# A new order of units, output halves, softmax pieces and bands in the first four blocks of a fused dynamic convolution and squared-ReLU feed-forward kernel

## Chip, cores and metric

The kernel runs on one core of one Trainium2 chip. The metric is the device time of one execution in microseconds (us). In the profile lines PE is TensorE, ACT ScalarE, DVE VectorE and POOL GpSimd.

## The reference

```python
w = softmax(weight_gen, axis=-1)          # (8, 4096, 8 heads, 7 taps)
x_pad = pad x (8, 4096, 192) with 6 zero rows in front
y[b, s, h, :] = sum_k w[b, s, h, k] * x_pad[b, s + k, h, :]   # 24 channels a head
h = maximum(y.reshape(32768, 192) @ w_in, 0)                  # w_in 192 x 2048
out = (h * h) @ w_out                                         # w_out 2048 x 192
```

## The kernel before

The 32768 rows are cut into sub-blocks of 512 rows. Blocks 0 and 1 are one sub-block each, all later blocks are two. For each block there are these kinds of work:

- **Softmax pieces** give the taps: an exponential on ScalarE ("E"), then sum, reciprocal and scaling on VectorE ("S"). The inputs come in numbered parts; "part 1's weights" below are the softmax inputs of part 1, not weights of the feed-forward. The taps of small parts are moved into the row layout by DMA ("row moves"); those of large parts go through a buffer v_big, which is cleared once.
- **Bands** ("B"): VectorE spreads the taps of a sub-block over a band matrix, so that the convolution is a matmul.
- **Convolution** ("C"): TensorE multiplies x with the bands into one or two tiles "yp", and ScalarE casts them to y.
- **Units** ("u"): the first matmul of 2 x 512 values into a tile h of PSUM (three such buffers, shared with yp), a relu on ScalarE into t (five buffers), a square on VectorE into g.
- **Halves** ("M"): a quarter is 256 rows of out, and a half is half of its second matmul. After the second half ScalarE copies the sum out, and if the quarter used two banks, VectorE adds the second bank.

W_in and w_out are the weights of the two matmuls. In the traces each engine does its work in program order: in run 1 below, for instance, a relu whose unit had ended at 18.90 us began only at 21.93, behind an exponential that stood before it and waited 1.25 us for its weights. So the order written in the program is the schedule. In blocks 0 to 3 it was this:

```python
orders = {0: "uuuuuCuuu", 1: "MuMuuuMuuuMCu", 2: "MuuuuMuuuuMuuuuuuuMCu"}
steady = "MuMuuu" * 3 + "MuuuMCu"          # from block 3 on
# softmax pieces and bands hang on a unit: (block, unit)
at(0, 4, "exp", s1, 0, s1.rh)
at(0, 5, "soft", s1, 0, s1.rh)
...
st_conv(0)
st_bands(1)
x_cast(1, nc.vector.tensor_copy)
nc.gpsimd.memset(x_st[1][:, 0:1], 0.0)     # a gate: waits for the cast of x
for q in range(4):
    load_w_out(q, 4)
s2.load(nc.gpsimd)
nc.gpsimd.memset(v_big, 0.0)
...
for j, (sub, n) in enumerate(BLOCKS):
    u = m = 0
    for step in orders.get(j, steady):
        if step == "M":                    # a half of block j - 1
            qt, part = divmod(m, 2)
            m += 1
            if part == 0:
                o = new_o(ps_o, 1 if j < 3 else 2)   # one bank (128 rows) or two (64 rows each)
            st_mm2(j - 1, qt, FCS[part], (0, 1), o)
            if part == 1:
                o_sum(j - 1, qt, (0, 1), o)
                ...
        elif step == "u":
            run_fill(j, u)
            st_unit(j, u)
            u += 1
        elif j + 1 < NBLK:
            st_conv(j + 1)
    if j == 0:
        x_load(2)                          # on GpSimd's queue, behind the row moves
        x_load(3)
```

The softmax here doesn't subtract the row's maximum and nothing guards it: scores larger than these inputs give would overflow.

## Time and profile before

| | before |
|---|---|
| median time, 3 runs | 751.88 us (751.43 to 752.27) |
| profiled span | 749.2 us |
| TensorE busy | 739.0 us (99%) |
| VectorE, ScalarE busy | 621.8 and 623.0 us (83% each) |
| mean granted clock | 1.000 |
| blocks 0 to 4 begin at | 15.47, 24.14, 38.92, 57.66, 80.59 us |

"Busy" of TensorE counts a matmul that waits inside a group (7 units of block 2 count as 5.55 us of work without a gap, where they take 4.5 at the price of 0.65 each), so 99% does not mean that nothing is lost. What is lost shows when the starts of the blocks are compared with the price of the work in them. The prediction below does this and prints the lines. Two words of the profile: "<-" in brackets names what ended a wait, and "issue" is a wait for which the profile shows no cause.

### The profile page before, as it was taken

Reading aid. Unit: us, or ns where it says so; the run is one execution under the profiler, and the core shown is the slowest. Engines: PE = TensorE matmul, PEld = TensorE weight load, DVE = VectorE, ACT = ScalarE, POOL = GpSimd, SP = SyncE. Lnnn points to the kernel's source line nnn. Section 1 sums busy time; section 2 is a strip of 40 time slices with the busy share of each in tenths; the row PEclk is TensorE's granted clock in tenths of the full one; section 3 lists DMA queues with packets and bytes.
Section 4 is the critical chain, followed back from the end, with each engine's and each line's share of the span. In section 5 each row is a group of like instructions: output and inputs, shape, how many; then the busy total and the mean of one; then the engine's idle time right before and its main releaser. Section 6 shows DMA issues by size and latency. Waiting matters only on the chain.

```text
span 749.2 us, 33282 instructions
## 1 busy us (share of the span) xinstructions
PE 739.0 (99%) x15106; PEld 559.8 (75%) x15106; DVE 621.8 (83%) x1001; ACT 623.0 (83%) x753; POOL 87.9 (12%) x127
## 2 busy tenths in 40 slices
PE   8899999999999999999999999999999999999998
PEld 4658777777887777777877777777778777777787
DVE  5889998998789888887888888898888987677853
ACT  4898888888888888888888888888888888888883
POOL 3522220001101000011000110001100011001000
PEclk9999999999999999999999999999999999999999
DMA  8846444446453344543245442365441354441312
GB/s 231 129 74 135 79 68 109 101 78 138 93 109 69 74 77 80 131 86 65 46 80 139 86 80 49 55 138 108 59 79 47 57 109 80 59 75 50 50 45 65
DMA packets 122329, 65.20 MB, mean 87 GB/s; under 512 B 83881, under 2 KB 118668, under 8 KB 121676
## 3 DMA queue, kind: packets, MB, share of 16 engines
q1 hardware_dynamic: 77868, 46.05, 22.4%
q0 software_dynamic: 44176, 16.93, 20.6%
q8 instruction: 118, 1.93, 1.1%
q14 instruction: 23, 0.19, 0.1%
q10 hardware_dynamic: 144, 0.10, 0.0%
HBM read 48.61 MB, written 28.70 MB: 103 GB/s over the span
## 4 chain that ended last, share of the span: by engine, by line
PE 88%; DVE 5%; DMA 3%; ACT 1%; issue 1%; SPq 0%; POOL 0%; DVEq 0%; ACTq 0%
PE o L453 42%; PE h L419 40%; PE yp L394 6%; DVE g L431 2%; DVE bd L326 1%; DMA xt<-in_x_dram 1%; ACT t L428 1%; DMA x_st<-in_x_dram 1%; DMA vd<-v_big 1%; DVE v_first L217 1%; DVE ssum L202 0%; DVE rcp L209 0%; DMA wg<-in_weight_gen_dram 0%; DVE o_sb L469 0%; POOL wr L308 0%
## 5 line engine op out<-in xcount | busy, mean ns | idle before, releaser
L428 ACT ACTIVATE t<-h 128x1024 f16<-128x1024 f32 x512 | 497.1, 1027 | 66.9 <-PE h L419 66.6
L431 DVE TENSOR_TENSOR g<-t 128x1024 f16<-128x1024 f16 x512 | 334.5, 687 | 101.9 <-ACT t L428 99.1
L453 PEld LDWEIGHTS <-g 64*128 64x128 f16 (+1 forms) x8032 | 353.0, 94 | 55.7 <-issue 5.0
L453 PE MATMUL o<-w_o,g 64*128 64x192 f16 (+1 forms) x8032 | 386.1, 243 | 1.7 <-DMA w_o<-in_moe_w_out_dram 0.7
L419 PE MATMUL h<-y,w_i 64*128 64x512 f16 (+1 forms) x3168 | 379.8, 370 | 2.1 <-ACT t L428 0.9
L419 PEld LDWEIGHTS <-w_i 64*128 64x128 f16 x3168 | 165.5, 94 | 114.7 <-issue 5.0
L326 DVE TENSOR_TENSOR bd<-wr,mask 128x4160 f16<-128x4160 f16 (+3 forms) x89 | 149.4, 1702 | 4.6 <-DMA wr<-v_first 4.6
L278 POOL DMA_DIRECT2D xt<-in_x_dram x62 | 51.3, 832 | 446.1 <-PE yp L394 422.8
L467 ACT COPY o_sb<-o 128x384 f32<-128x384 f32 x129 | 62.3, 483 | 33.2 <-PE o L453 33.2
L469 DVE TENSOR_TENSOR o_sb<-o,o_sb 128x384 f32<-128x384 f32 x123 | 68.2, 554 | 8.0 <-ACT o_sb L467 5.6
L405 ACT CAST y<-yp 128x1024 f16<-128x1024 f32 (+1 forms) x64 | 48.2, 803 | 16.5 <-PE yp L394 16.5
L394 PE MATMUL yp<-bd,xt 128*32 128x104 f16 (+8 forms) x3864 | 52.0, 208 | 1.8 <-DMA xt<-in_x_dram 1.2
L394 PEld LDWEIGHTS <-xt 128*32 128x32 f16 (+3 forms) x3864 | 46.1, 91 | 8.0 <-issue 6.4
L217 DVE TENSOR_TENSOR v_big<-ex,rcp 128x112 f16<-128x112 f32 (+1 forms) x136 | 27.3, 263 | 1.8 <-DMA vd<-v_big 0.6
L195 ACT ACTIVATE ex<-wg 128x448 f32<-128x448 f32 (+2 forms) x44 | 27.2, 618 | 1.9 <-DMA wg<-in_weight_gen_dram 1.9
L202 DVE TENSOR_REDUCE ssum<-ex 128x64 f32<-128x448 f32 (+2 forms) x44 | 26.1, 593 | 2.4 <-ACT ex L195 2.4
L209 DVE RECIPROCAL rcp<-ssum 128x64 f32<-128x64 f32 (+2 forms) x44 | 23.7, 539 | 1.5
L268 POOL DMA_DIRECT2D xt<-in_x_dram x7 | 3.8, 547 | 136.9 <-PE yp L394 136.9
L308 POOL DMA_DIRECT2D wr<-v_first x31 | 16.8, 562 | 15.4 <-DVE v_first L217 15.3
L516 PE MATMUL wp<-warm 128*128 128x512 f16 x42 | 11.1, 432 | 1.3 <-DVE warm L508 1.3
L516 PEld LDWEIGHTS <-warm 128*128 128x128 f16 x42 | 4.5, 109 | 7.4 <-issue 2.5
L217 DVE TENSOR_TENSOR v_first<-ex,rcp 128x112 f16<-128x112 f32 (+1 forms) x48 | 9.1, 255 | 0.3
(19 smaller groups left out, 24.5 us busy)
## 6 DMA issues: line engine op xcount, KB each, us to landing
out_dram<-o_sb SPq DMA_DIRECT2D x63, 384.0 KB, 2.9
xt<-in_x_dram POOLq DMA_DIRECT2D x42, 240.0 KB, 6.0
wg<-in_weight_gen_dram SPq DMA_DIRECT2D x4, 1064.0 KB, 7.7
xt<-in_x_dram POOLq DMA_DIRECT2D x20, 192.0 KB, 5.6
wr<-vd SPq DMA_DIRECT2D x38, 80.0 KB, 5.0
vd<-v_big SPq DMA_DIRECT2D x5, 512.0 KB, 5.5
wg<-in_weight_gen_dram SPq DMA_DIRECT2D x5, 392.0 KB, 4.2
wg<-in_weight_gen_dram SPq DMA_DIRECT2D x3, 616.0 KB, 5.5
```

What stands on the lines that cost most here:

```text
L195: nc.scalar.activation(out=self.ex[:, lo:hi].rearrange("p r g k e -> p (r g) k e"), in_=self.wg[:, lo:hi].rearrange("p r (g e) k -> p (r g ...
L217: eng.tensor_tensor(out=bass.AP(tensor=v.tensor, offset=v.offset + lo * H * SL + lo % SL * 2 + g * SL * 2, ap=[list(v.ap[0]), [H * SL + 2, ...
L278: eng.dma_start(out=dst[:, first:last], in_=ap)
L326: nc.vector.tensor_tensor(out=bd_t[j][:, H * lo : H * (lo + len(tiles) * n)].rearrange("p (g m c) -> p g m c", g=shape[1], c=2 * SL), in0= ...
L394: nc.tensor.matmul(out=yps[k // per][p0 : p0 + m, col + a : col + b], lhsT=x_t[s][:, i, 32 * q : 32 * q + m], rhs=bd[:, h // 2, h % 2, a - ...
L405: nc.scalar.copy(out=y[:, k0:k1, 0:th], in_=yp[:, 0 : (k1 - k0) * th].rearrange("p (k c) -> p k c", c=th),)
L419: nc.tensor.matmul(out=h[:, half, jj * th : (jj + 1) * th], lhsT=w_in_chunk(u * per + jj, slot, half), rhs=y_t[j][r0 : r0 + RT, k, 0:th], ...
L428: nc.scalar.activation(out=t1, in_=h, func=ActF.Relu)
L431: nc.vector.tensor_tensor(out=g, in0=t1, in1=t1, op=AluOp.mult)
L453: nc.tensor.matmul(out=oo[:, cc * Dm : (cc + 1) * Dm], lhsT=g[r0 : r0 + n, cc * P : (cc + 1) * P], rhs=w_o[r0 : r0 + n, fc, :], start=(fc ...
L467: nc.scalar.copy(out=o_sb, in_=o[0][:, c])
L469: nc.vector.tensor_tensor(out=o_sb, in0=o[1][:, c], in1=o_sb, op=AluOp.add)
```

## The change

The intent: ScalarE is full in block 0, idle for 4 us in block 1, and full again in block 2. A written-out plan for each of blocks 0 to 3 spreads the halves so that TensorE has other work while ScalarE catches up, and brings the softmax forward so that bands are ready. E, S, B and L (a load of softmax inputs) are now steps of the plan, with the number of the part or sub-block. Quarters of blocks 0 and 1 take banks o0 and o1 in turn. x for block 2 is requested before the row moves where it can be. The clearing of v_big moves to the start, and the gate reads x instead of overwriting it.

```diff
-def new_o(pool, banks=2):
+def new_o(pool, banks=2, first=0):
...
         band_mask()
+        nc.gpsimd.memset(v_big, 0.0)
...
-        st_bands(1)
-        x_cast(1, nc.vector.tensor_copy)
-        nc.gpsimd.memset(x_st[1][:, 0:1], 0.0)
+        nc.gpsimd.tensor_copy(out=gate, in_=x_st[1][:, 0:1])
         for q in range(4):
             load_w_out(q, 4)
         s2.load(nc.gpsimd)
-        nc.gpsimd.memset(v_big, 0.0)
-        orders = {0: "uuuuuCuuu", 1: "MuMuuuMuuuMCu", 2: "MuuuuMuuuuMuuuuuuuMCu"}
+        x_load(2)
         steady = "MuMuuu" * 3 + "MuuuMCu"
+        plans = {
+            0: "B1 X1 u u u E1 S1 u C u u u u",
+            1: "L3 u u B2 M E2 B3 u M E2 u u S2 u M u C u S2 M",
+            2: "L4 u u u E3 M u u u M B4 u u u u M B5 S3 u u u u M u E3 C u",
+            3: "L5 L6 M S3 u u u M u u u u M u M B6 E4 u u u M M B7 u u S4 u E4 M u C M u",
+        }
...
+                    o = new_o(ps_o, 1, qt % 2) if j < 2 else new_o(ps_o)
...
                     st_conv(j + 1)
+                    if j == 0:
+                        x_load(3)
+                    elif j + 2 < NBLK: ...      # x of block j + 2, right behind the convolution
```

## The prediction

> **What bounds the kernel now.** I read the page first. TensorE is busy nearly always, ScalarE and VectorE each five sixths of the time, and the clock is full throughout:
>
> ```profile
> span 749.2 us, 33282 instructions
> PE 739.0 (99%) x15106; PEld 559.8 (75%) x15106; DVE 621.8 (83%) x1001; ACT 623.0 (83%) x753; POOL 87.9 (12%) x127
> ```
>
> So the end is set by TensorE's work plus what it loses, and the loss is small. To find where it sits I read the timeline of TensorE (start, length, instructions; the gap before in brackets), since a matmul group that waits inside still counts as busy. These lines start a block or show a loss ("o" is the second matmul, "yp" the convolution, "h" the first matmul):
>
> ```profile
> 15.47 3.88 PE L419 MATMUL h<-y,w_i 64*128 64x256 f16 x60 [0.89 <-ACT y L405]
> ...
> 24.14 1.48 PE L453 MATMUL o<-w_o,g 128*128 128x192 f16 x16 [0.72 <-DMA w_o<-in_moe_w_out_dram]
> ...
> 36.65 1.58 PE L394 MATMUL yp<-bd,xt 128*32 128x104 f16 x118 [1.05 <-DMA xt<-in_x_dram]
> 38.16 0.83 PE L419 MATMUL h<-y,w_i 64*128 64x256 f16 x12
> 38.92 1.49 PE L453 MATMUL o<-w_o,g 128*128 128x192 f16 x16
> ...
> 48.59 5.55 PE L419 MATMUL h<-y,w_i 64*128 64x512 f16 x42
> ...
> 57.66 1.48 PE L453 MATMUL o<-w_o,g 64*128 64x192 f16 x32
> ...
> 80.59 1.48 PE L453 MATMUL o<-w_o,g 64*128 64x192 f16 x32
> ```
>
> Blocks 0 to 4 thus begin at 15.47, 24.14, 38.92, 57.66 and 80.59 us; block 5 begins at 103.12. From the same timeline come TensorE's unit prices where nothing waits, as differences of starts: a unit of the first matmul 0.65 us (18 matmuls, three units, 1.94 in the chain); a half of the second matmul 1.32 us with 64 rows and 1.41 with 128 rows (24.14 to 25.55); a convolution 1.51 us for a double block (55.50 to 57.01), 0.88 for block 1's (19.28 to 20.16). Floors against what was used:
> - block 0: 8 x 0.65 + 0.88 = 6.1; used 8.67, lost 2.6
> - block 1: 8 x 0.65 + 4 x 1.41 + 1.51 = 12.35; used 14.78, lost 2.4
> - block 2: 16 x 0.65 + 4 x 1.41 + 1.51 = 17.55; used 18.74, lost 1.2
> - block 3: 16 x 0.65 + 8 x 1.32 + 1.51 = 22.5; used 22.93, lost 0.4
> - block 4: the same floor; used 22.53, lost nothing.
>
> The change can only win from these 6.6 us. Now ScalarE's timeline, because block 0 has no second matmul for TensorE to do beside ScalarE:
>
> ```profile
> 16.34 3.77 ACT L428 ACTIVATE t<-h 128x1024 f16<-128x1024 f32 x4 [0.92 <-PE h L419]
> 19.97 0.96 ACT L195 ACTIVATE ex<-wg 128x784 f32<-128x784 f32 x1
> 20.79 1.05 ACT L428 ACTIVATE t<-h 128x1024 f16<-128x1024 f32 x1
> 21.70 0.84 ACT L405 CAST y<-yp 128x768 f16<-128x768 f32 x1
> 22.37 2.92 ACT L428 ACTIVATE t<-h 128x1024 f16<-128x1024 f32 x3
> 26.42 1.02 ACT L428 ACTIVATE t<-h 128x1024 f16<-128x1024 f32 x1 [1.13 <-PE h L419]
> ...
> 37.84 1.50 ACT L405 CAST y<-yp 128x1024 f16<-128x1024 f32 x2 [1.72 <-PE yp L394]
> ```
>
> From 16.34 to 25.29 ScalarE never rests: a relu costs it 0.91 us back to back (four in 3.77), more than TensorE's 0.65 per unit, and with three h buffers TensorE must follow. Block 0's loss is therefore ScalarE's and stays. In block 1 it is reversed: ScalarE rests 1.13 us while TensorE does second matmuls, 0.78 and 0.29 around the first output copy, and 1.72 while the convolution of block 2 waits for x. Those 4 us of ScalarE are missing in block 2, where it is again full and 7 units take 5.55 us instead of 4.5. The last part of the evidence is the chain of waits: after the row moves comes
>
> ```profile
> 28.78 7.83 DMA xt<-in_x_dram x2
> 36.65 1.17 PE yp L394 x67
> ```
>
> [...] ScalarE is full in block 0, TensorE from block 3 on. [...] The trace shows 6.4 to 6.5 us from issue to landing, which I use. [...]
>
> **The change part by part.** No compute work is added or removed except one 1-column memset that becomes a copy; everything is order.
>
> *Clearing v_big earlier* (one 2.50 us memset, 22.29): it goes behind the mask, which GpSimd ends at about 3.73, so it ends near 6.3; GpSimd is next needed at 8.65. Free.
>
> *The gate.* The old memset waited for VectorE's cast of x (18.24); the copy needs only the landed x (17.4). w_out, the weights of part 2 and x for sub-block 2 move 0.8 us ahead. The 0.72 us wait for w_out at 24.14 vanishes, also because two units now come first.
>
> *First softmax piece one unit earlier.* Its weights are issued at 14.39 and land 5.2 us later, 19.6. The new slot on ScalarE is 19.1 (third relu starts at 18.17). So I expect a new wait of 0.5 us, pushing block 0's last relu end from 25.29 to about 25.8. In return VectorE takes the sum, reciprocal and scaling (0.97 + 0.85 + 1.46 and gaps, 3.3 us) at 20.6 instead of 22.48: done at 23.9 instead of 25.8, and the bands of block 2 about 2 us earlier.
>
> *Block 1.* Two units first, the second waiting for ScalarE's relu near 24.85: ends 25.5. Then half 26.9, unit 27.55, half 28.95, two units 30.25, unit 30.9, half 32.3, unit 32.95: each step from the prices above, and at each ScalarE (0.91 per relu, 0.5 per copy or exponential) keeps up. Now the convolution. x for sub-block 2 is early (issued near 21.5, landed by 28). x for sub-block 3 must wait for block 1's convolution and, in GpSimd's order, stands behind the row moves, which end at 23.9 + 0.3 + 2.7 = 26.9; a 0.6 us request precedes its main one at 27.5, which lands 6.4 us later, 33.9. So 0.95 us of wait remains instead of 1.24 counted from a later point. Convolution to 35.4, unit 36.05, half 37.45. The kernel before has the same eight units, four halves and convolution done at 38.92. Gain so far 1.5 us.
>
> *Block 2.* ScalarE has 16 x 0.91 + 1.5 (casts) + 1.1 (exponentials) + 1.0 (copies) = 18.2 us, and its queue runs up to three buffers behind TensorE, so TensorE can nearly keep its floor 17.55: end 37.45 + 17.55 = 55.0 (before 57.66). VectorE's share (16 x 0.61, two band pairs at 2.33 + 2.35, two softmax pieces at 2.0 and 1.7) is about 18.2 too: fits, with no slack.
>
> *Block 3.* Halves are spread where ScalarE needs them: 22.5 to 22.6, end 77.6. From there nothing differs but the x request before the row moves, and no later convolution waits for x.
>
> *Two banks in turn.* They free a quarter's first matmul from the previous output copy. In the trace no quarter of blocks 0 and 1 waits for that copy (units lie between), so by itself this is worth 0.
>
> Sum: 80.59 - 77.6 = 3.0 us, carried to the end, since TensorE is full from there.
>
> **The rivals.**
> 1. *All of it is won.* If ScalarE doesn't wait for part 1's weights and x for sub-block 3 is in time, 1.4 us more: gain 4.4, time 747.5. [...] Against: both landings are measured, and neither issue is early enough.
> 2. *VectorE or ScalarE becomes the bound of blocks 2 and 3.* Both have 18.2 us of work against 17.55, and VectorE is 97% busy from 80 to 125 us. A band that comes late because the next pieces of softmax stand ahead of it would stall a convolution by 1 to 2 us: gain 1, time 750.9. For: in-order queues without slack. Against: five t buffers and 28 g buffers decouple them, and ScalarE enters block 2 about 2 us ahead of before.
> 3. *The lead is given back later*, by a later wait that does not move with the start (blocks 5 and 6 show vd landing in the chain at 126.75): time 751.9. Against: those transfers are issued by the same shifted engines, and the blocks there run at TensorE's floor.
>
> **Range and chances.** I take the sum, less 0.2 us for gaps at hand-overs: 2.8 of 751.88 gives 749.1. The 80% range goes from rival 1, 747.4, to a little past rival 2, 751.0. A change of 2% is 15 us, more than twice the whole loss of 6.6, so faster by over 2% has 0.01; slower by over 2% needs a new stall of a kind not seen here, 0.01.
>
> **What will show it.** Right: block 3's end (the start of the first second matmul of block 4) near 77.6; ScalarE waiting about 0.5 us for the weights before its second exponential; a wait for x of about 1 us ahead of block 2's convolution near 33; no w_out wait; ScalarE's rest in block 1 down from 4 us to about 2. Wrong: any wait over 1 us on TensorE after 38 us, a block 2 longer than 18.3, or later blocks longer than 22.55.

The 6.4 to 6.5 us are from request to landing of the 192 and 240 KB of x asked for from 28.78 us on. That the clearing of v_big is free rests on GpSimd's gap up to 8.65 us alone.

## More of the kernel before

W_in is cast by ScalarE and then copied across partitions by DMA (its "crossing").

## The result

| | before | changed |
|---|---|---|
| median, 4 runs each | 751.65 us (751.18 to 752.27) | 750.67 us (750.16 to 751.45) |
| ratio, 95% interval | | 0.9987 (0.997 to 1.0005) |
| unedited repeat, later | 752.42 us, 11 runs | 750.93 us, 5 runs |
| ratio, 95% interval | | 0.9983 (0.9969 to 0.9997) |

A ratio is the mean time of one kernel's runs over that of the other's of the same rounds, so it is not quite the ratio of the medians. The time lies within the predicted range (747.4 to 751.0), but the gain is 1.0 to 1.3 us by the ratios and not the 2.8 that the point of 749.1 stood for. It is barely apart from the noise: the first interval includes 1.

The timeline of TensorE in the changed kernel, at the stages that answer to the lines of before:

```profile
16.82 5.30 PE L419 MATMUL h<-y,w_i 64*128 64x256 f16 x48 [0.89 <-ACT y L405]
...
27.92 1.50 PE L453 MATMUL o<-w_o,g 128*128 128x192 f16 x16
...
35.78 1.58 PE L394 MATMUL yp<-bd,xt 128*32 128x104 f16 x120
...
39.49 2.12 PE L419 MATMUL h<-y,w_i 64*128 64x512 f16 x18
41.54 1.49 PE L453 MATMUL o<-w_o,g 128*128 128x192 f16 x16
...
57.60 1.48 PE L453 MATMUL o<-w_o,g 64*128 64x192 f16 x32
58.92 2.11 PE L419 MATMUL h<-y,w_i 64*128 64x512 f16 x18
60.86 1.48 PE L453 MATMUL o<-w_o,g 64*128 64x192 f16 x32
...
80.23 0.24 PE L453 MATMUL o<-w_o,g 64*128 64x192 f16 x1
81.08 1.48 PE L453 MATMUL o<-w_o,g 64*128 64x192 f16 x31 [0.61 <-DVE o_sb L469]
```

The waits for w_out and for x are gone. Two things are new. Block 0's first unit came 1.35 us later than before (16.82 against 15.47) and its 48 matmuls took 5.30 us; and at 80.23 a half stops after one matmul for VectorE's add of the two output banks. ScalarE's rests in block 1, 4 us before, are these (the last lies at the start of block 2):

```profile
31.63 0.48 ACT L467 COPY o_sb<-o 128x384 f32<-128x384 f32 x1 [0.37 <-PE o L453]
...
35.90 1.02 ACT L428 ACTIVATE t<-h 128x1024 f16<-128x1024 f32 x1 [0.63 <-PE h L419]
...
39.59 0.48 ACT L467 COPY o_sb<-o 128x384 f32<-128x384 f32 x1 [0.22 <-PE o L453]
```

The view by stretches says why the 48 matmuls were slow, 5.30 us against 2.79 in the repeat at a clock of 1.00 (columns: stretch, its length, busy time of TensorE, weight loads, VectorE, ScalarE, GpSimd with counts, granted clock, DMA share, GB/s):

```profile
12.00:14.00 2.00, 0.75 (x26) 0.41 (x25) 1.38 (x3) 1.47 (x1) 0.49 (x1) 1.00 0.92 227
14.00:15.60 1.60, 1.21 (x64) 0.83 (x50) 1.60 (x4) 0.00 (x0) 0.00 (x0) 0.87 0.83 219
15.60:22.00 6.40, 5.51 (x61) 4.19 (x51) 3.97 (x6) 3.96 (x5) 4.60 (x7) 0.50 1.07 198
22.00:24.00 2.00, 2.00 (x92) 1.68 (x92) 1.83 (x3) 2.00 (x3) 0.10 (x1) 1.00 1.49 172
```

From 15.2 to 22.0 us the granted clock is one half (finer stretches put the fall at 15.17). Before the fall TensorE had rested 0.97, 0.28 and 0.28 us since 12.3; the rest of 0.89 ahead of the first unit came after it. That these rests brought the clock down is not shown. The three profiles in which TensorE rested 0.73 us or more between its warm-up matmuls and the first bands (0.97 here, 0.89 in run 5, 0.73 in run 12) had the half clock right after; the others rested at most 0.55 there and did not. Here the half clock lasted 6.83 us. In seven of the twelve profiles of the new order the clock fell once, and it stayed at half for 3.41 us (four profiles) or 6.83 us (three); in the two profiles of the old order it never fell.

Because the start moves from run to run, stages are counted here from block 0's first unit; what this hides is told below the table. The repeat of the changed kernel had its first unit at 16.11 us and a full clock (1.00):

| us after block 0's first unit | predicted | before | changed | changed, repeat |
|---|---|---|---|---|
| first half of block 1 | 10.0 | 8.67 (two units fewer ahead of it) | 11.10 | 11.08 |
| convolution for block 2 | 18.4 | 19.90, with 1.24 of wait inside | 18.96 | 18.94 |
| block 2 begins | 22.0 | 23.45 | 22.67 | 22.65 |
| block 3 begins | 39.5 | 42.19 | 40.78 | 40.77 |
| block 4 begins | 62.1 | 65.12 | 63.41 | 63.40 |
| convolution inside block 4 | | 85.49 | 84.62 | 84.62 |

In the text, "block 2's convolution" is the one for block 2 (inside block 1), and "block 4's convolution" is the one inside block 4. So 1.7 us are won up to block 4, and 0.87 up to block 4's convolution. From there both kernels run the same program, and the next convolution follows after 22.53 us in both. From block 2's convolution to block 4's the kernel before took 65.59 us and the changed one 65.66: what blocks 2 and 3 win, block 4 gives back, and the net gain lies ahead of block 2's convolution.

0.87 us is near the measured 1.0 to 1.3, but these profiles do not prove that it is the same gain:

- The three profiled executions took 751.43 (before), 751.45 and 751.62 us (changed), so they differ by nothing like 0.87. In the first the later start ate the gain. In the repeat the start ate 0.64, and from 123.26 to 146.53 us (23.27, against 22.82 before) 0.45 us more was lost, with a short wait at 126.36.
- Counting from the first unit flatters a late start, because part 1's weights land at about the same time of the execution whether the first unit is early or late (20.1 to 21.8 us where ScalarE waited for them). Of the twelve profiles with the new order, each with its edit, the six whose first unit came before 16 us have block 4's convolution 85.25 to 87.71 us after it, the six with a later one 83.94 to 85.46; the old order has 85.49 and 85.53, with early starts. Counted from the start of the execution it stands at 100.71 to 102.81 us with the new order and at 100.96 and 100.64 with the old.

### The profile page after: what moved, and what is told of

It reads as the page before. It is cut to its first block, busy times and chain, and to the rows that moved or that the text cites. A ratio compares the mean times of both kernels' runs of the same rounds, so it can differ in the third digit from the quotient of the medians.

```text
span 749.6 us, 33285 instructions
## 1 busy us (share of the span) xinstructions
PE 740.7 (99%) x15106; PEld 560.6 (75%) x15106; DVE 621.9 (83%) x1001; ACT 623.5 (83%) x753; POOL 87.9 (12%) x127
## 3 DMA queue, kind: packets, MB, share of 16 engines
q0 software_dynamic: 44176, 16.93, 20.3%
## 4 chain that ended last, share of the span: by engine, by line
PE 94%; DVE 2%; DMA 1%; issue 1%; ACT 1%; DVEq 0%; ACTq 0%
PE o L453 45%; PE h L419 44%; PE yp L394 6%; DVE bd L326 1%; DVE g L431 1%; DMA wr<-v_first 1%; ACT t L428 0%; DMA wg<-in_weight_gen_dram 0%; DVE v_first L217 0%; ACT ex L195 0%; DVE ssum L202 0%; DVE rcp L209 0%; DVE o_sb L469 0%; ACT y L405 0%; ACT o_sb L467 0%
## 5 line engine op out<-in xcount | busy, mean ns | idle before, releaser
L394 PE MATMUL yp<-bd,xt 128*32 128x104 f16 (+7 forms) x3864 | 52.1, 208 | 1.6 <-DVE bd L326 1.5
```

Source lines behind the costliest of these rows:

```text
L394: nc.tensor.matmul(out=yps[k // per][p0 : p0 + m, col + a : col + b], lhsT=x_t[s][:, i, 32 * q : 32 * q + m], rhs=bd[:, h // 2, h % 2, a - ...
```

## The experiments

Twelve kernels ran. All gave the reference's result. The kernel before ran beside each group, on the same chip.

**1. The changed kernel again** (no edit).

> The changed kernel once more, unedited. Theory A (the profiled execution had a bad start: W_in landed 1.1 us later than in the kernel before and the clock was at half from 16 to 22 us): a profile with a good start has its first unit near 15.5 us, the clock at 1.00 in all stretches, block 4 beginning 2 to 3 us earlier than the kernel before (near 78), and the time 1.3 to 2 us under the kernel before. Theory B (the late start belongs to the change, for instance by the early clearing of v_big): first unit again near 16.8 us, W_in landing again after 8.3 us, half clock again.

Measured: 750.93 us, ratio 0.9983. First unit at 16.11, W_in's cast at 7.66 (7.24 before, 8.39 in the first profile), clock 1.00 throughout. So the half clock does not come in every execution, but the stage table shows the same 11.08. The timeline of ScalarE tells where that time went here:

```profile
16.98 2.85 ACT L428 ACTIVATE t<-h 128x1024 f16<-128x1024 f32 x3 [0.92 <-PE h L419]
21.08 0.94 ACT L195 ACTIVATE ex<-wg 128x784 f32<-128x784 f32 x1 [1.25 <-DMA wg<-in_weight_gen_dram]
```

ScalarE does three relus and then stands 1.25 us at the exponential of part 1, whose weights were requested at 14.50 us and landed 6.6 us later. In the first profile the start was so late that these weights were there in time. Two different losses of about 1.4 us (against the 9.72 of run 4, which had neither) thus gave the same 11.1; that they agree is luck. Theory A holds for the clock, but block 4 began at 79.51 and not near 78.

**2. v_big cleared late.**

```diff
-        nc.gpsimd.memset(v_big, 0.0)      # behind the mask
         ...
         s2.load(nc.gpsimd)
+        nc.gpsimd.memset(v_big, 0.0)
```

> v_big cleared where it was before, after the weights of part 2; else as changed. Theory B (the early memset slows the first transfers): W_in's cast on ScalarE starts near 7.2 us instead of 8.4, and the time is 1 us under the changed kernel of the same rounds. Theory A (chance): start spread as in the changed kernel, time the same within 0.3 us, or 0.2 to 0.5 later because x for sub-block 2 waits behind the memset.

Measured: 751.26 us, ratio 0.998 (0.9965 to 0.9995), mean time 0.2 us under the repeat's, which is within the noise. First unit at 15.54. With the early clearing the first unit came between 15.10 and 15.53 in six profiles and between 16.11 and 16.93 in six others. An early start is thus possible with it. Whether it makes late starts likelier, two profiles with the late clearing cannot tell. This profile also shows how much block 0 varies: ScalarE waited 2.24 us for part 1's weights, the clock was at half for 3.41 us from 22.91, and block 4's convolution came 86.35 us after the first unit, later than in the kernel before.

**3. The old order with everything else changed.** The four plans spell out the old order, for instance

```diff
-1: "L3 u u B2 M E2 B3 u M E2 u u S2 u M u C u S2 M"
+1: "M L3 u M B2 u u E2 B3 u M u E2 u u M C S2 u"
```

> The changed kernel with the order of units, halves, softmax pieces and bands of the kernel before in blocks 0 to 3; banks in turn, gate, early clearing and early x remain. If the gain is the order's: the time is that of the kernel before less at most 1.2 us (the wait for x before block 2's convolution goes). If it is x's alone: equal to the changed kernel within 0.3 us.

Measured: 752.0 us, ratio 0.9993 (0.998 to 1.0007). Block 4's convolution starts 85.53 us after the first unit, against 85.49 before. The wait for x is gone, but the convolution for block 2 waits 0.64 us for its bands instead:

```profile
36.09 1.84 PE L394 MATMUL yp<-bd,xt 128*32 128x104 f16 x118 [0.64 <-DVE bd L326]
```

So banks, gate, early clearing and early x show no gain without the order. That the gain is the order's fits this, and fits the ratios: of the twelve measurements of kernels with the new order in blocks 1 and 2, nine lie below 0.9993, with a middle value of 0.9982. It is not shown: this interval overlaps that of the repeat (0.9969 to 0.9997), and three kernels with the new order (runs 6, 8 and 11) did no better than 0.9993.

**4. The last half of block 3 ahead of the convolution.**

```diff
-3: "... M M B7 u u S4 u E4 M u C M u"
+3: "... M M B7 u u S4 u E4 M u M C u"
```

> The changed kernel with the last half of the second matmul of block 3 put before block 4's convolution instead of after it. Theory: in the changed kernel block 4's first half waits 0.6 us for the sum of the two output banks (VectorE's add at 80.5), because only one unit lies between; here convolution and unit lie between, so that wait goes and the time is 0.4 to 0.7 us under the changed kernel. Rival (VectorE is behind by then, the wait only moves to the next band or sum): no difference, within 0.2 us.

Measured: 751.21 us, ratio 0.9981, no different from the repeat, and TensorE still waits 0.70 us. The rival holds. VectorE's part of the timeline shows the queue in front of the add:

```profile
73.09 2.35 DVE L326 TENSOR_TENSOR bd<-wr,mask 128x3328 f16<-128x3328 f16 x2
75.35 1.29 DVE L431 TENSOR_TENSOR g<-t 128x1024 f16<-128x1024 f16 x2
76.56 0.61 DVE L202 TENSOR_REDUCE ssum<-ex 128x64 f32<-128x448 f32 x1
77.21 0.55 DVE L209 RECIPROCAL rcp<-ssum 128x64 f32<-128x64 f32 x1
77.80 0.83 DVE L217 TENSOR_TENSOR v_first<-ex,rcp 128x112 f16<-128x112 f32 x4
78.55 1.29 DVE L431 TENSOR_TENSOR g<-t 128x1024 f16<-128x1024 f16 x2
79.75 0.55 DVE L469 TENSOR_TENSOR o_sb<-o,o_sb 128x384 f32<-128x384 f32 x1
```

There is no gap from the band to the add: a softmax piece of 2.0 us stands between them. This profile also shows block 0 without either loss (full clock, weights in time): the first half of block 1 came 9.72 us after the first unit, where the prediction had 10.0 with its half us of wait. The weights were in time because the first unit was late, at 16.77 us.

**5. The softmax piece behind the last half.**

```diff
-3: "... M M B7 u u S4 u E4 M u C M u"
+3: "... M M B7 u u u E4 M u C M S4 u"
```

> The changed kernel with the first softmax piece of part 4 moved behind the last half of block 3, as the kernel before had it. Theory (the traces of the changed kernel and of end3 show VectorE without a gap from block 3's last band to the add of the two output banks at 79.8, so the 2.0 us piece queued ahead of that add is what block 4's first half waits for): the 0.6 us wait of TensorE on VectorE's add before block 4's second half goes, block 4's convolution starts 0.6 to 0.9 us earlier after block 0's first unit than in the changed kernel, time 0.5 us less. Rival (the piece's 2 us only come later on VectorE and stall a later sum or block 4's bands): a wait of the same size elsewhere in block 4, time the same.

Measured: 751.0 us, ratio 0.9976 (0.9948 to 1.0003). From block 2's convolution to block 4's it took 65.54 us, against 65.66 to 65.68 in the changed kernel: 0.1 us and not 0.6. VectorE now stands idle before the add, and the wait has another cause:

```profile
79.97 0.56 DVE L469 TENSOR_TENSOR o_sb<-o,o_sb 128x384 f32<-128x384 f32 x1 [1.65 <-ACT o_sb L467]
```

With only one unit (0.65 us) between the end of a quarter and the next quarter, copy (0.48) and add (0.56) behind each other do not fit, and TensorE waits 0.35 us. Neither theory had the whole of it. (Here too the clock was at half for 6.83 us, from 14.70.)

**6. The exponential and softmax of part 1 where they were.**

```diff
-0: "B1 X1 u u u E1 S1 u C u u u u"
+0: "B1 X1 u u u u E1 u C S1 u u u"
```

> The changed kernel with the exponential of part 1 after four units and its softmax after block 1's convolution, as before. Theory (in four of five profiles with the early place ScalarE or TensorE lost 0.9 to 1.9 us there, because part 1's weights had not landed): ScalarE's wait for the weights is at most 0.4 us, TensorE's wait on the relu in block 0 falls from 1.5 to 0.5 to 0.9 us; the bands of block 2 come 1 to 2 us later but x isn't awaited, so block 4's convolution starts 0.5 us earlier after the first unit. Rival: the later bands delay the convolution of block 2, and nothing or up to 1 us is lost.

Measured: 752.51 us, ratio 0.9999. ScalarE still waited 1.6 us for the weights (landed at 21.4), TensorE waited 1.6 us for W_in, and then the convolution for block 2 waited 1.4 us for its bands, which the later softmax had delayed. The rival holds. All six times lie between 752.17 and 753.76, and the mean is 1.5 us above that of run 5 in the same rounds: the early place is the better one, and what fails is the landing.

**7. Part 1's weights requested earlier.**

```diff
-        cross_w_in(1)
         s1.load(nc.sync)
+        cross_w_in(1)
```

> The changed kernel with part 1's weights requested ahead of the second crossing of W_in (which waits for ScalarE's cast), so about 1.4 us earlier. If the landing of these weights is what ScalarE waits for: no wait before the second exponential, TensorE's wait on the relu in block 0 at most 0.9 us, block 4's convolution 0.6 to 1.5 us earlier after the first unit than in the changed kernel, time 0.5 to 1 us less. If the transfers only share the same rate: the crossing lands later, TensorE waits for W_in instead, and nothing is won.

Measured: 750.64 us, ratio 0.9973 (0.9948 to 0.9999). Requested at 12.67 instead of about 14.4, the weights landed at 20.36, after 7.7 us; ScalarE waited 0.39. But block 1's convolution stopped 1.99 us on "issue", the clock fell (0.57 from 22 to 23 us, then 0.50), and the first half of block 1 came at 11.92. The request moved about 1.8 us ahead and the landing by 0.1 to 1.5 us (20.43 to 21.82 in the other profiles of the new order where ScalarE waited); whether the transfers share a rate was not tested. The ratio is the lowest, though its interval includes the ratios of all the others; the profiled execution was the slowest of its six, so what the early request does in a fast one was not seen.

**8. x requested late.**

```diff
         s2.load(nc.gpsimd)
-        x_load(2)
...                                        # and x_load(3): both at the end of block 0
+            if j == 0:
+                x_load(2)
+                x_load(3)
```

> The changed kernel with both x requests of block 2 after the row moves, as before; the order stays new. If the early request is worth what the old wait of 1.2 us suggests: TensorE waits 0.5 to 1.5 us for x before block 2's convolution and the time is 0.5 to 1 us over the changed kernel. If the new order gives x enough time by itself (the convolution of block 2 now has no wait on x at all in any profile): no wait, or under 0.3 us, time the same.

Measured: 752.1 us, ratio 0.9993 (0.9967 to 1.0018). No wait for x; the longest waits of TensorE are others:

```profile
PE h L419 <- ACT t L428: 1.7, 1, 1.7
PE yp L394 <- DVE xt L292: 1.1, 1, 1.1
PE h L419 <- ACT y L405: 0.9, 1, 0.9
```

The second line is the cast of block 1's x, not a wait for block 2's. The profile fell on a bad start: part 1's weights came 3.0 us late and the clock was at half for 6.82 us from 21.36, which moved everything behind them and gave x that much more time. From block 2's convolution to block 4's the kernel took 65.68 us, as the changed one. So the early request is not shown to be worth anything; an execution with a good start could still need it.

**9. The old gate, and both edits at block 3's end.**

```diff
-        nc.gpsimd.tensor_copy(out=gate, in_=x_st[1][:, 0:1])
+        st_bands(1)
+        x_cast(1, nc.vector.tensor_copy)
+        nc.gpsimd.memset(x_st[1][:, 0:1], 0.0)
...
-0: "B1 X1 u u u E1 ..."
+0: "u u u E1 ..."
-3: "... M M B7 u u S4 u E4 M u C M u"
+3: "... M M B7 u u u E4 M u M C S4 u"
```

> Two edits of the changed kernel that act 60 us apart and are read apart. First, the gate is the old memset again, which waits for VectorE's cast of x, so w_out's transfers start at about 18.8 us instead of 17.5 to 18.4. If w_out's early transfers hold up part 1's weights (they landed 6.6 to 7.5 us after issue in the four changed variants where ScalarE waited for them, 5.2 in the kernel before): landing again 5 to 6 us after issue, ScalarE's wait for them at most 0.6 us. Rival (chance of the start): landing still over 6.5. Second, in block 3 the last half stands before the convolution (as in end3) and the softmax piece behind it (as in s4_last). Each alone left TensorE waiting 0.7 and 0.35 us for the add of the output banks, with two different releasers (VectorE's queue in end3, the copy and add themselves in s4_last); together: no such wait, block 4's convolution 0.6 us nearer to block 2's. Time 0.5 to 1.5 us less than the changed kernel.

Measured: 750.26 us, ratio 0.9979 (0.9962 to 0.9997). The first theory falls: w_out was requested from 19.06 us on, and part 1's weights still took 6.6 us and held ScalarE for 1.71 (the clock then fell to half for 3.41 us). The second holds. The end of block 3 runs through:

```profile
76.81 1.50 PE L453 MATMUL o<-w_o,g 64*128 64x192 f16 x32
78.25 1.58 PE L394 MATMUL yp<-bd,xt 128*32 128x104 f16 x120
79.76 0.82 PE L419 MATMUL h<-y,w_i 64*128 64x512 f16 x6
80.42 1.48 PE L453 MATMUL o<-w_o,g 64*128 64x192 f16 x32
```

No wait for the add is left anywhere, and block 2's convolution to block 4's took 65.01 us, 0.65 less than in the changed kernel (0.4 to 0.6 less than with the old order).

**10. Idle matmuls in block 0.**

```diff
+        idle = ps_o.tile([P, TB], f32, name="o1")
+        def keep(n):
+            for i in range(n):
+                nc.tensor.matmul(out=idle, lhsT=warm[:, 0:P], rhs=warm, start=True, stop=True)
+        keep(3)                            # behind block 0's convolution
...
                     st_unit(j, u)
+                    if j == 0:
+                        keep(1)
```

> The changed kernel with idle matmuls (512 columns, 0.22 us each, into an output bank not yet in use, never read): three after block 0's convolution, one after each unit of block 0. If TensorE's rests in block 0 are what takes the clock to half in the changed order (10 of 15 runs of the changed kernel and its x- and v_big-variants show a mean clock of 0.998 or less, 2 of 11 of the kernel before): the clock is 1.00 in every stretch after 12 us and at least 0.999 in nearly all runs; the time falls 0.3 to 1 us. If the clock follows something else: the same share of runs below 0.999, time the same or up to 0.5 us more.

Measured: 750.49 us, ratio 0.9979 (0.9964 to 0.9994). The mean clock was 1.00 in all six runs, and they lay within 0.9 us of each other (749.94 to 750.84). Without the idle matmuls, 37 of the 57 runs of the kernels with the new order had a mean clock of 0.998 or less, and so had 14 of 44 runs of the kernel before in the four groups of runs. (The expectation's counts do not come out: the changed kernel and its x- and v_big-variants had 13 of 21, the kernel before 5 of 22 in the first two groups.) This fits the expectation's first case, that TensorE's rests take the clock down, but does not show it: run 12 with the same idle matmuls had a half clock in its profile and two of six runs under 0.999. The matmuls are not free: a unit and its idle matmul follow each other at 1.08 us (16.57 to 17.65), above ScalarE's 0.91 per relu, and the first half of block 1 came at 12.18, with 1.55 us of wait for the weights in it.

**11. One bank for blocks 0 and 1.**

```diff
-                    o = new_o(ps_o, 1, qt % 2) if j < 2 else new_o(ps_o)
+                    o = new_o(ps_o, 1) if j < 2 else new_o(ps_o)
```

> The changed kernel with blocks 0 and 1 using one output bank for all quarters, as before. Theory of the prediction (two banks in turn are worth 0, since units always lie between a quarter's end and the next quarter's start): no wait of TensorE on the output copy in blocks 1 and 2, time the same within noise. Rival: in block 2 the halves stand three and four units apart on a full ScalarE, the copy comes late and the next quarter waits 0.3 us or more, twice.

Measured: 751.39 us, ratio 0.9993 (0.9974 to 1.0012). No wait on the output copy. The halves of block 2 stand at

```profile
41.57 1.49 PE L453 MATMUL o<-w_o,g 128*128 128x192 f16 x16
...
45.05 1.49 PE L453 MATMUL o<-w_o,g 128*128 128x192 f16 x16
...
49.17 1.49 PE L453 MATMUL o<-w_o,g 128*128 128x192 f16 x16
```

3.48 and 4.12 us apart. In the repeat of the changed kernel these spacings are 3.47 and 4.13 us (40.81, 44.28, 48.41). Banks in turn are worth nothing here. The 0.92 us that this profile lost ahead of block 2's convolution was a wait for bands, whose row moves had landed late.

**12. Three repairs together**: the idle matmuls of 10, block 3's end of 9, and part 1's weights requested by GpSimd behind the first row moves.

```diff
         wr_load_sbuf(1, [s0], range(NT), (nc.gpsimd,))
+        s1.load(nc.gpsimd)
```

> Three repairs of the changed kernel together, each read at its own stage: idle matmuls in block 0 (as in warm), block 3's end as in gate_old_end, and part 1's weights requested by GpSimd right behind the first row moves, near 12.5 us instead of 14.4, with the crossing of W_in left alone. If the landing of part 1's weights decides the wait in block 0: ScalarE's wait before the second exponential at most 0.4 us (1.6 in warm), block 1's first half of the second matmul 1 us or more nearer to block 0's first unit than the 11 to 12.4 us of the changed variants. Clock at 0.999 or more in all runs, no wait on the add of the output banks. Sum: 2 to 2.5 us under the kernel before, times between 748.5 and 750.5. Rival: the earlier request takes its bytes from x for block 1, the cast and block 1's convolution come later by as much, and the time stays at warm's 0.9979 of the kernel before.

Measured: 750.65 us, ratio 0.9985 (0.9969 to 1.0). The time is the rival's. The weights were in time, and x for block 1 came later: the gate, which waits for it, opened at 20.13 us, against 17.4 to 18.7 in the other profiles with this gate. But the rival's path is not seen: the cast of x was done by 20.9, and block 1's convolution began at 21.95 without a wait. What the profile shows ahead of it is a half clock from 15.05 to 18.47 us and the idle matmuls. The clock fell before the first idle matmul ran (15.54), so in this profile they came too late to prevent it; TensorE had rested 0.73, 0.28 and 0.28 us ahead of that. The first half of block 1 came at 11.61. The wait for the add was gone. Two of six runs still had a mean clock under 0.999. No version beats the changed kernel by more than the noise.

## Why the prediction was right, and where its steps were not

The time fell into the range, with a gain under half of the point's. The direction of the mechanism is seen in the traces: ScalarE's rest in block 1 fell from 4 us to about 1.2 (0.37, 0.63 and 0.22 in the first profile), the waits for w_out and x went, and blocks 2 and 3 became shorter (18.11 and 22.63 us, from 18.74 and 22.93). That the order, through this, makes the 1.0 to 1.3 us is argued and not shown (run 3, and the points below the stage table). Of the prediction's own signs of being right, two came (no wait for w_out, ScalarE's rest down) and three did not (block 3's end near 77.6: 80.23 and 79.51; a wait of 0.5 us for the weights: none and 1.25; a wait for x of about 1 us: none). Of its signs of being wrong one came: block 4 took 23.37 us, more than 22.55. The range's upper end, 751.0, stood for a gain of only 0.9 us, and the time scatters by more than its distance from 750.67: that it fell inside is partly luck. Step by step, from the stage table:

- *"The new slot on ScalarE is 19.1 ... a new wait of 0.5 us."* This term failed most: the first half of block 1 came 1.1 us later than predicted. The 0.5 rested on a single landing, 5.2 us after the request, at 19.6. In the profiles of runs 1, 2, 6, 8, 9, 10 and 11 ScalarE waited 1.2 to 3.0 us. Where a late start let the weights come in time (the first profile), the half clock took as much. With a late start and full clock (run 4) the stage was even 0.3 us earlier than predicted.
- *"0.95 us of wait remains"* for x: there was none. Block 1 reached its convolution later than assumed (18.94 us after the first unit), and x had landed. This gave back part of the first error.
- *The unit prices.* Block 2 took 18.11 us and not 17.55. The price of 0.65 holds beside halves of 64 rows: three units take 1.94 us in block 3 (58.92 to 60.86). Beside halves of 128 rows they take 2.05 (39.49 to 41.54). Blocks 1 and 2 have only such halves, so in block 2 of this order five groups of units cost 0.1 us each that the floor of 17.55 left out. By this price, fewer and longer groups would pay less; no run tried them. What causes the 0.1 us no run isolates. The prediction's own lines held the dearer price: from 38.16 to 38.92 one unit takes 0.76.
- *Block 3*: predicted 22.5 to 22.6, measured 22.63. Right.
- *"From there nothing differs."* Wrong by 0.84 us, the difference between the gain at block 4's start and at its convolution. The softmax piece queued ahead of the add (run 4) and the single unit after the last half (run 5) each hold block 4 back, and only both edits together free it (runs 9 and 12). This was rival 2's kind of loss, a VectorE without slack, at a place that it did not name.
- *"Worth 0"* for two banks in turn: right (run 11). The clearing of v_big as *free* is neither shown nor refuted (run 2). In the kernel before, the old clearing (22.29 to 24.79 us) ran beside the softmax sum at 22.48 and the reciprocal at 23.48, which took 0.96 and 0.85 us, as they do without it (0.97 and 0.85 at 4.99 and 5.99). The gate moved w_out ahead as told, and the wait for w_out went.

The sum: 3.0 predicted, less 1.1 in block 0, plus 0.4 in block 1, less 0.6 in block 2 and 0.8 in block 4, is 0.9, the measured 0.87.

What stays open: whether the measured gain is the order's; and why part 1's weights land after 5.2 us in some executions and 7.7 in others. The timing of w_out's requests is not the cause by itself (run 9), and an earlier request brought no gain that the runs can tell from the changed kernel's (runs 7 and 12). Open too is a wait of 0.5 to 2.0 us on "issue" inside block 1's convolution, always before its last 11 matmuls, in five profiles of the new order.

## What to carry to other kernels

Near the start, count stages from the first unit that every version shares; the end time mixes a gain of one us with a start that scatters by two (15.10 to 16.93 us here). But compare them from the start of the execution too: transfers do not wait for the first unit, so a late start hides a wait for them (none for part 1's weights with the first unit at 16.77 and 16.82 us in run 4 and the first profile, 1.25 us at 16.11 in run 1). One profile of each kernel is then too few. A wait that depends on one DMA landing needs several profiles before it gets a number, and an engine that works in program order should not be given work that waits on such a landing in front of work that is ready (1.25 us of ScalarE in run 1). When pieces are pulled forward on one engine, check what they now stand in front of: here a softmax piece of 2.0 us delayed an add of 0.56 us that TensorE was waiting for.
